# ScalarE's copies of gathered rows placed later, an expert's first two tiles transposed on TensorE, and the gate weights loaded first on their queue

## The chip, the cores and the metric

The kernel runs on one core of one Trainium2 chip. The metric is the device time of one execution in microseconds (us). Engines: TensorE (PE) multiplies and transposes, VectorE (DVE) and ScalarE (ACT) work element by element, GpSimd (POOL) pools early batches and issues gathers and scatters, SyncE (SP) issues DMAs. Each runs its own list of instructions strictly in order; they wait for each other through semaphores.

## The reference, cut to what matters

```python
k_p = k.reshape(B, H, Sp, 8, D).mean(axis=3)          # B = 8 batches, H = 8 heads, S = 576 rows, D = 64
v_p = v.reshape(B, H, Sp, 8, D).mean(axis=3)
attn = softmax(scale * q @ k_p.T);  a = attn @ v_p    # per batch and head
x = a.transpose(0, 2, 1, 3).reshape(4608, 512)
logits = x @ w_gate                                   # 8 experts
# greedy: (token, expert) pairs by falling logit; a token goes to the first expert
# with room for it, 576 tokens each
for e in range(8):
    out[mask_e] = np.maximum(x[mask_e] @ w1[e], 0.0) @ w2[e]    # w1 512 x 1024, w2 1024 x 512
```

## The kernel before, in words

**Attention.** The 4608 rows are 36 tiles of 128. For a tile, PE forms the scores (`st_s`, L229), transposes the exponentials (`st_e`, L258) and multiplies them with the values (`st_av`, L271). Keys and values of a batch are pooled beforehand: for batch 0 by PE and DVE, for the others by POOL (L174 to L178 for keys, L187 to L197 for values). Beside the pooled values stands a block of logits: `prep_v` transposes the sums of values (L210) and ACT copies them as `vT` (L212), `prep_g` multiplies `vT` with the gate weights `wblk` (L219), and DVE puts the product into `vblk` (L220). So every attention tile needs `wblk` through its batch's `prep_g`. `wblk` is 44 KB; its load is the last step of `local()` (L114, L115), on ACT's DMA queue, behind ACT's setting of constants. The rows go to `xd` in DRAM.

**Routing.** For one expert after another a search finds which tokens it takes: rounds of DVE comparing (L601), PE counting (L644), DVE diagonal and count (L648, L652), PE (L656), DVE (`g`, L663), PE (L670), DVE (`up`, L672). At the end of a search come the rows as indices (L740). The rounds are laid among the products of the expert before, at places that a planner chooses; since PE and DVE run in order, a round that is late stops what stands behind it.

**Experts.** An expert takes 576 tokens, four tiles of 128 and one of 64. Each fp32 factor is split in a high and a low part (`xh`, `xl`, `w1h`, `w1l`, `hh`, `hl`, `w2h`, `w2l`; ACT rounds the high part, DVE subtracts), and three products stand for one. Stage 1 (L1081) goes over the 8 blocks of 128 hidden columns twice: for tokens 0 to 255, then for tokens 256 to 575; a block is 12 matmuls, after which ACT takes `hh` (L1086), in the second pass `hr` too (L1088), and DVE takes `hl` (L1089). Stage 2 (L1115) has four tiles of 24 matmuls and a half tile (L1120); ACT evicts them as `yt` (L1129) and `yh` (L1133), POOL scatters them (L1095). ACT also makes `w1h` (L1033) and `w2h` (L1043) in eight pieces each, DVE `w1l` (L1037) and `w2l` (L1046).

**Gathered rows.** An expert's rows come from `xd` by POOL's indirect DMA, one per tile (`fetch`, L996), and must be transposed. For expert 0 they land in `xg` and PE transposes them, four transposes a tile (L1057), from whose PSUM tile `tp` ACT takes `xh` (L1059) and DVE `xl` (L1061). For experts 1 to 7 they land in one of three buffers `xa`; ACT copies them to `xg` with their 16-bit halves apart (`split`, L1004), SP transposes that by DMA back into `xa` (L1006), ACT puts the halves together (`join`, L1013), and then come `xh` (L1025, ACT) and `xl` (L1026, DVE).

**What sets the order.** `experts()` writes the program while it keeps an estimated clock `now`, in us. `at(after, f)` puts a step on the list `moves`, which `move(until)` empties in turn as the clock reaches each; `later` does the same for DVE. `gather` plans splits and joins at fixed distances from the moment the rows are known: splits 0 to 2 at 5.0 + 1.3t, joins 0 to 2 at 11.0 + 1.3t, the fetches of tiles 3 and 4 with joins 0 and 1, splits 3 and 4 at 13.0 + 1.3t, joins 3 and 4 at 20.0 + 1.3t. `turns` and `turn` place `xh` and `xl` of a tile from 20.0 + 1.5t on. For experts 3 to 7 the rows are known during stage 1 of the expert before; for expert 1 this is during stage 2 of expert 0.

Of the kernel before, what the change touches and what calls it, by code (L numbers as in the profile page):

```python
# [9 lines left out]
F32 = mybir.dt.float32  # L10
# [13 lines left out]
class Attention:  # L24
# [44 lines left out]
    def local(self, loc, full, consts, more, then):  # L69
        nc = self.nc  # L70

        self.kblk = [loc.tile([128, 4, 144], F32, name=f"kblk{i}") for i in range(4)]
        nc.gpsimd.memset(self.kblk[0], 0.0)

        row = loc.tile([128, 1], I32, name="row")
        nc.gpsimd.iota(row, pattern=[[0, 1]], base=0, channel_multiplier=1)
        edges = loc.tile([128, 16], F32, name="edges")
        at = []
        n = 0
        for _, heads in self.CHUNKS:  # L80
            at.append(n)
            for e in (*(h[1] for h in heads), heads[-1][2]):
                nc.gpsimd.memset(edges[:, n:n + 1], float(e))
                n += 1
        rowf = loc.tile([128, 1], F32, name="rowf")
        nc.vector.tensor_copy(rowf, row)
        nc.vector.tensor_tensor(edges, rowf.to_broadcast([128, 16]), edges, op=OP.is_ge)
        self.mask = loc.tile([128, 11], F32, name="mask")
        for c, n in enumerate(at):
            b0, b1 = self.BLOCKS[c:c + 2]  # L90
            nc.vector.tensor_tensor(self.mask[:, b0:b1], edges[:, n:n + b1 - b0], edges[:, n + 1:n + 1 + b1 - b0],
                                    op=OP.subtract)

        ones = loc.tile([128, 11], F32, name="ones8")
        nc.vector.tensor_scalar(ones, self.mask, 8.0, None, op0=OP.mult)
        small = loc.tile([128, 1], F32, name="small")
        nc.vector.tensor_scalar(small, rowf, 127.0, 8e-9, op0=OP.is_ge, op1=OP.mult)
        for b in (slice(0, 2), slice(3, 5), slice(6, 9), slice(10, 11)):
            nc.vector.tensor_scalar(ones[:, b], ones[:, b], small, None, op0=OP.add)

        self.eTs = [loc.tile([128, 5, 128], F32, name=f"eT{i}") for i in range(3)]
        for t in self.eTs:
            nc.scalar.activation(t[96:], full[96:, None, :].to_broadcast([32, 5, 128]), AF.Copy)
        self.vblk = [loc.tile([128, 11, 73], F32, name=f"vblk{i}") for i in range(4)]
        for t in self.vblk:
            nc.scalar.activation(t[:, :, 72], ones, AF.Copy)
        for t in self.kblk[1:]:
            nc.scalar.activation(t.rearrange("p j (a y) -> p (j a) y", a=2), full[:, None, :72].to_broadcast([128, 8, 72]),
                                 AF.Copy, scale=0.0)
        consts()  # L110
        then()
        more()

        self.wblk = loc.tile([128, 88], F32, name="wblk")  # L114
        nc.scalar.dma_start(self.wblk, self.wb)  # L115

    def load_k(self, b, halves=(slice(0, 4),)):
        self.rk[b] = self.raw.tile([128, 4, 8, 72], F32, name="rawk", bufs=3)
# [806 lines left out]
class Experts:  # L925
# [46 lines left out]
    def rows_of(self, t):  # L972
        return min(128, self.cap - 128 * t)

    def gather(self, rows, at=None):

        self.xg = self.buf("xg", [128, 5, 512])
        if at is None:
            for t in range(5):
                self.fetch(rows, t, self.xg[:, t])  # L980
            return
        self.xa = self.buf("xa", [128, 3, 512])
        for t in range(3):
            self.fetch(rows, t, self.xa[:, t])
            at(5.0 + 1.3 * t, lambda t=t: self.split(t))
        for t in range(2):
            at(11.0 + 1.3 * t, lambda t=t: (self.join(t), self.fetch(rows, t + 3, self.xa[:, t])))
        at(13.6, lambda: self.join(2))
        for t in range(3, 5):
            at(13.0 + 1.3 * t, lambda t=t: self.split(t))  # L990
        for t in range(3, 5):
            at(20.0 + 1.3 * t, lambda t=t: self.join(t))

    def fetch(self, rows, t, to):
        n = self.rows_of(t)
# [192 lines left out]
def experts(ctx, tc, g, R, xd, w1, w2, out, ident, cap, keep):  # L1188
# [13 lines left out]
    def later(after, t, f):  # L1202

        waiting.append((now + after, t, f))

    moves = []

    def at(after, f):
# [14 lines left out]
    def step(e):  # L1223
# [5 lines left out]
        if what == "id":  # L1229

            if p > e or p and pieces[p - 1].l < 8:
                held.append((p, crit, t, what))
                return False
            X.load_1(R.eid, 0, 4 if p else 2)
            eids[p] = R.eid
        elif what == "rows":
            if p and turned[p - 1] < 5:
                held.append((p, crit, t, what))
                return False
            X.gather(R.rows, at if p else None)  # L1240
            toks[p] = R.rows, R.halves
            turned[p] = 0
        since[p, what] = now
# [46 lines left out]
    def turn(e, t, name="tp", bufs=2):  # L1290

        nonlocal now
        if e:
            now = max(now, since[e, "rows"] + 20.0 + 1.5 * t)
            move(since[e, "rows"] + (11.0, 12.3, 13.6, 23.9, 25.2)[t])
            flush(1)
            X.xt_joined(t, later)
        else:
# [7 lines left out]
    def turns(e, upto, t0):  # L1306

        nonlocal last
        t = turned.get(e, 5)
        if t < upto and due(e, "rows", 20.0 + 1.5 * t if e else 6.5 + 1.3 * t) and now >= last + 1.4:  # L1310
            last = now
            turn(e, t)

# [158 lines left out]
```

## Time and profile before

| | |
|---|---|
| time, median of 3 runs (lowest to highest) | 625.4 us (624.82 to 625.49) |
| the profiled execution's own time | 625.91 us |
| its span, first to last instruction | 624.1 us |
| mean granted TensorE clock in it | 0.973 |
| attention | about 0 to 135 us |
| routing of expert 0, with PE mostly idle | about 139 to 163 us |
| experts | about 165 us to the end |

The profile is of one execution. A row of a timeline gives start, duration, engine, line, operation, the tiles written and read, and how many such instructions follow each other; in brackets stands how long the engine was idle before it, and what ended that. Durations of successive instructions overlap a little, so that the distance between starts is what an instruction takes of its engine. `PEld` is the loading of weights, which runs beside PE; an engine's name with a q is the part that issues DMAs and waits. A row of the windows gives, for a stretch of time, each engine's busy time and instructions, then the granted TensorE clock (1.00 is full speed), the busy share of the DMA engines and GB/s. A row of the chain gives start, duration, and what the end of the program was then waiting for. All lines are those of the kernel before.

### The profile page before, as it was taken

What the parts mean: (1) busy time and instruction counts of PE and PEld (TensorE: products, weight loads), DVE (VectorE), ACT (ScalarE), POOL (GpSimd) and SP (SyncE); (2) the same over time, 40 slices, a digit from 0 to 9 for tenths busy, and PEclk for the clock granted to TensorE, in tenths of its full rate; (3) what the DMA queues carried; (4) which work ended last, traced back from release to release, by engine and by line L of the source; (5) the groups of instructions that cost most, each with busy time, mean ns of one, the idle gap of its engine ahead of it and who ended that gap; (6) DMA issues with size and microseconds to landing.
All of it is one profiled execution on the core that took longest, in us unless ns stands there. A gap on an engine that the chain in (4) does not pass through costs nothing.

```text
span 624.1 us, 11279 instructions
## 1 busy us (share of the span) xinstructions
PE 585.8 (94%) x4155; PEld 509.4 (82%) x4155; DVE 394.1 (63%) x1149; ACT 305.0 (49%) x624; POOL 175.3 (28%) x219
## 2 busy tenths in 40 slices
PE   7899999995799989999899989998999999999994
PEld 5899999884498769878877987897789889979972
DVE  7477777888886677877674776377647616615300
ACT  7244444442353475663844294248327925925310
POOL 2999998000300420322102211111212111120021
PEclk9799999996899989999999989999999999999997
DMA  8999982121640873637611941383156228314011
GB/s 355 421 379 356 396 304 86 69 78 59 211 137 1 264 201 102 179 91 252 170 43 52 328 95 42 107 287 72 50 212 195 60 100 301 80 52 162 2 43 39
DMA packets 65986, 100.38 MB, mean 161 GB/s; under 512 B 36848, under 2 KB 36864, under 8 KB 63232
## 3 DMA queue, kind: packets, MB, share of 16 engines
q1 hardware_dynamic: 54672, 71.18, 34.6%
q0 software_dynamic: 5920, 18.89, 8.6%
q10 hardware_dynamic: 5328, 9.48, 4.1%
q8 instruction: 35, 0.57, 0.4%
q14 instruction: 31, 0.25, 0.1%
HBM read 72.40 MB, written 18.87 MB: 146 GB/s over the span
## 4 chain that ended last, share of the span: by engine, by line
PE 71%; issue 10%; DMA 7%; ACT 5%; DVE 3%; POOL 1%; POOLq 0%; another core or an unknown queue 0%; SPq 0%; DVEq 0%; ACTq 0%
PE h L1115 23%; PE h L1081 22%; PE psa L271 8%; PE pss L229 6%; DMA xa<-xd,rows 3%; PE h L1120 3%; PE pse L258 2%; ACT xg L1004 2%; PE rt L258 1%; DMA wblk<-in_moe_w_gate_dram 1%; DMA xg<-xd,rows 1%; PE rt L219 1%; PE rt L644 1%; ACT hh L1086 1%; PE rt L505 1%
## 5 line engine op out<-in xcount | busy, mean ns | idle before, releaser
L1115 PE MATMUL h<-w2l,hh 128*128 128x512 f32 x256 | 101.8, 398 | 0.0
L1115 PE MATMUL h<-w2h,hl 128*128 128x512 f32 x256 | 101.6, 397 | 0.0
L1115 PE MATMUL h<-w2h,hh 128*128 128x512 f32 x256 | 100.6, 393 | 0.3 <-PEq L1179 0.3
L1081 PE MATMUL h<-xh,w1h 128*128 128x320 f32 (+1 forms) x512 | 93.3, 302 | 2.6 <-ACT xh L1025 2.0
L1081 PE MATMUL h<-xl,w1h 128*128 128x320 f32 (+1 forms) x512 | 95.3, 303 | 0.0
L1081 PE MATMUL h<-xh,w1l 128*128 128x320 f32 (+1 forms) x512 | 91.0, 300 | 0.0
L1086 ACT ACTIVATE hh<-h 128x320 fp32r<-128x320 f32 (+1 forms) x128 | 53.0, 416 | 77.0 <-PE h L1081 68.9
L1095 POOL DMA_INDIRECT out_dram<-yt,rows x29 | 29.2, 1006 | 200.0 <-ACT yt L1129 199.6
L1089 DVE SCALAR_TENSOR_TENSOR hl<-h,hh 128x320 fp32r<-128x320 f32 (+1 forms) x128 | 57.5, 453 | 42.6 <-ACT hr L1088 23.3
L1081 PEld LDWEIGHTS h<-xh,w1h 128*128 128x128 f32 x512 | 76.4, 192 | 6.1 <-issue 3.1
L1081 PEld LDWEIGHTS h<-xl,w1h 128*128 128x128 f32 x512 | 77.8, 192 | 2.3 <-issue 2.3
L1081 PEld LDWEIGHTS h<-xh,w1l 128*128 128x128 f32 x512 | 76.6, 192 | 0.1
L996 POOL DMA_INDIRECT xa<-xd,rows x35 | 35.1, 1002 | 135.0 <-ACT xg L1013 64.4
L1129 ACT ACTIVATE yt<-h 128x512 f32<-128x512 f32 x32 | 19.2, 599 | 96.9 <-PE h L1115 62.5
L271 PE MATMUL psa<-vblk,eT 128*128 128x146 f32 (+3 forms) x400 | 63.0, 305 | 0.0
L1026 DVE TENSOR_TENSOR xl<-xg,xh 128x512 fp32r<-128x512 f32 (+1 forms) x35 | 22.0, 630 | 54.1 <-ACT xh L1025 54.1
L1115 PEld LDWEIGHTS h<-w2h,hh 128*128 128x128 f32 x256 | 48.2, 188 | 9.6 <-issue 0.7
L1115 PEld LDWEIGHTS h<-w2h,hl 128*128 128x128 f32 x256 | 48.2, 188 | 9.0
L1115 PEld LDWEIGHTS h<-w2l,hh 128*128 128x128 f32 x256 | 48.4, 189 | 8.6
L271 PEld LDWEIGHTS psa<-vblk,eT 128*128 128x128 f32 (+1 forms) x400 | 53.1, 182 | 1.8 <-issue 0.3
L1046 DVE TENSOR_TENSOR w2l<-raw,w2h 128x512 fp32r<-128x512 f32 x64 | 43.2, 682 | 5.8 <-ACT w2h L1043 5.8
L1004 ACT ACTIVATE xg<-xa 128x1024 uint16<-128x1024 uint16 (+1 forms) x35 | 36.8, 1064 | 19.7 <-DMA xa<-xd,rows 18.6
(215 smaller groups left out, 957.3 us busy)
## 6 DMA issues: line engine op xcount, KB each, us to landing
raw<-in_moe_w_dram SPq DMA_DIRECT2D x64, 512.0 KB
xd<-xt ACTq DMA_DIRECT2D x36, 256.0 KB
rawv<-in_v_dram SPq DMA_DIRECT2D x7, 1280.0 KB
rawk<-in_k_dram SPq DMA_DIRECT2D x7, 1152.0 KB
rawq<-in_q_dram SPq DMA_DIRECT2D x7, 1152.0 KB
rawk<-in_k_dram SPq DMA_DIRECT2D x2, 576.0 KB
rawv<-in_v_dram SPq DMA_DIRECT2D x1, 768.0 KB
rawq<-in_q_dram SPq DMA_DIRECT2D x1, 640.0 KB
```

What stands on the lines that cost most here:

```text
L229: nc.tensor.matmul(ps[cols, j // 2, 144 * (j % 2):144 * (j % 2) + 144], self.q_of(b, j, n, cols.stop - cols.start), self.kblk[b % 4][:, j] ...
L271: self.nc.tensor.matmul(o[h], self.eT[i][:, c, h], self.vblk[b % 4][:, self.BLOCKS[c]:self.BLOCKS[c + 1]], start=(c == cs[0]), stop=(c == ...
L996: self.nc.gpsimd.indirect_dma_start(out=to[:n], out_offset=None, in_=self.xd, in_offset=bass.IndirectOffsetOnAxis(ap=rows[:n, t:t + 1], ax ...
L1004: nc.scalar.activation(xs.rearrange("p (s d) -> p s d", s=2), self.xa[:n, t % 3].bitcast(U16).rearrange("p (d s) -> p s d", s=2), AF.Copy)
L1026: later(0.9, 0.7, lambda: self.nc.vector.tensor_tensor(xl, x, xh.bitcast(F32), op=OP.subtract))
L1046: self.nc.vector.tensor_tensor(self.w2l[:, i], self.raw2[e][:, i], self.w2h[:, i].bitcast(F32), op=OP.subtract)
L1081: nc.tensor.matmul(ps[:, :m], a[:, j, fs], b[:, j, o], start=(n == 0), stop=(n == 11))
L1086: nc.scalar.activation(hh[:, f, o], ps[:, :m], AF.Relu)
L1089: later(0.65, 0.4, lambda f=f, o=o, m=m, ps=ps: nc.vector.scalar_tensor_tensor(hl[:, f, o], ps[:, :m], 0.0, hh[:, f, o].bitcast(F32), op0= ...
L1095: st = nc.gpsimd.indirect_dma_start(out=rows, out_offset=bass.IndirectOffsetOnAxis(ap=idx, axis=0), in_=y, in_offset=None)
L1115: nc.tensor.matmul(ps, a[:, f, o], b[:, f], start=(f == 0 and k == 0), stop=(f == 7 and k == 2))
L1129: self.nc.scalar.activation(y, ps, AF.Copy)
```

## The change

Three parts.

1. The tile `wblk` and its load move from the end of `local()` to its beginning.
2. `gather` is given the tiles that go `direct`: all five for expert 0, tiles 0 and 1 for expert 1, none for the others. Direct tiles are fetched into `xg` and transposed on PE. So expert 1 has eight more transposes on PE, and two splits, two DMA transposes and two joins fewer; its tiles 2 to 4 take the three buffers `xa`, and its five fetches are issued one behind the other.
3. For experts 2 to 7 splits 0 to 2 are planned at 10.0 + 1.4n, splits 3 and 4 at 25.0 and 26.5, and every join 6.5 behind its split. `joined` gives the time from which `xh` and `xl` of a tile may follow, and `turn` empties the list of planned steps up to that time. For expert 1 the three splits stand at 12.0 + 1.4n.

```diff
     def local(self, loc, full, consts, more, then):
         nc = self.nc
+
+        self.wblk = loc.tile([128, 88], F32, name="wblk")
+        nc.scalar.dma_start(self.wblk, self.wb)
...
         more()
 
-        self.wblk = loc.tile([128, 88], F32, name="wblk")
-        nc.scalar.dma_start(self.wblk, self.wb)
...
-    def gather(self, rows, at=None):
+    def gather(self, rows, direct=range(5), at=None):
 
         self.xg = self.buf("xg", [128, 5, 512])
-        if at is None:
-            for t in range(5):
-                self.fetch(rows, t, self.xg[:, t])
-            return
-        self.xa = self.buf("xa", [128, 3, 512])
-        for t in range(3):
-            self.fetch(rows, t, self.xa[:, t])
-            at(5.0 + 1.3 * t, lambda t=t: self.split(t))
-        for t in range(2):
-            at(11.0 + 1.3 * t, lambda t=t: (self.join(t), self.fetch(rows, t + 3, self.xa[:, t])))
-        at(13.6, lambda: self.join(2))
-        for t in range(3, 5):
-            at(13.0 + 1.3 * t, lambda t=t: self.split(t))
-        for t in range(3, 5):
-            at(20.0 + 1.3 * t, lambda t=t: self.join(t))
+        for t in direct:
+            self.fetch(rows, t, self.xg[:, t])
+        rest = [t for t in range(5) if t not in direct]
+        if rest:
+            self.xa = self.buf("xa", [128, 3, 512])
+        for t in rest[:3]:
+            self.fetch(rows, t, self.xa[:, t % 3])
+        plan = []
+        for n, t in enumerate(rest):
+            first = n < 3
+            begin = (10.0 if len(rest) > 3 else 12.0) + 1.4 * n if first else 25.0 + 1.5 * (n - 3)
+            plan.append((begin, lambda t=t: self.split(t)))
+            plan.append((begin + 6.5, lambda t=t: self.join(t)))
+            if first and n + 3 < len(rest):
+                plan.append((begin + 6.5, lambda t=rest[n + 3]: self.fetch(rows, t, self.xa[:, t % 3])))
+        for after, f in sorted(plan, key=lambda x: x[0]):
+            at(after, f)
+
+    @staticmethod
+    def joined(e, t):
+
+        return (26.0 - 1.5 * 3 + 1.5 * t if t > 2 else 10.0 + 1.4 * t) + 7.5 if e > 1 else 12.0 + 1.4 * (t - 2) + 7.5
...
+    def direct(e):
+        return range(5) if e == 0 else range(2) if e == 1 else range(0)
...
-            X.gather(R.rows, at if p else None)
+            X.gather(R.rows, direct(p), at)
...
-        if e:
-            now = max(now, since[e, "rows"] + 20.0 + 1.5 * t)
-            move(since[e, "rows"] + (11.0, 12.3, 13.6, 23.9, 25.2)[t])
+        if t not in direct(e):
+            now = max(now, since[e, "rows"] + X.joined(e, t))
+            move(now)
             flush(1)
...
-        if t < upto and due(e, "rows", 20.0 + 1.5 * t if e else 6.5 + 1.3 * t) and now >= last + 1.4:
+        if t < upto and due(e, "rows", 6.5 + 1.3 * t if t in direct(e) else X.joined(e, t)) and now >= last + 1.4:
```

How this moves instructions is shown at three places, all on ACT, whose rows PE and DVE wait for. Line numbers are each kernel's own: in the changed kernel the same statement stands 1 to 11 lines later (split L1012, join L1021, `xh` L1033 or from PSUM L1067, `w1h` L1041, `hh` L1094, `hr` L1096, `w2h` L1051, `yt` L1137, `yh` L1141). A number behind a tile's name is its buffer.

The first place is the start of the program on ACT, whose first rows set constants (`eT`, `vblk`, `kblk`). Before, the load of `wblk` stands behind all of them:

```order
L108 ACTIVATE kblk_131<-ones 128x576
L447 ACTIVATE j_190<-i_186 128x1152
L151 ACTIVATE kblk_128<-psa 64x72 x2
L483 ACTIVATE blk<-i_186 128x648
L484 ACTIVATE blk<-i_186 128x72
L115 DMA wblk<-in_moe_w_gate_dram 128x88
L241 ACTIVATE e<-e 128x576
```

In the changed kernel it is the first instruction behind the program's opening branch, ahead of the loading of ACT's table:

```order
L1479 UNCONDITIONAL_BRANCH
L73 DMA wblk<-in_moe_w_gate_dram 128x88
L106 ACT_TABLE_LOAD
L106 ACTIVATE eT_171<-ones 32x640
L106 ACTIVATE eT_172<-ones 32x640
```

Nothing else moves there, on ACT or on the other engines.

The second place is stage 2 of expert 0 on ACT, where expert 1's rows arrive. Before, behind two evictions `yt`:

```order
L1129 ACTIVATE yt<-h 128x512 x2
L1004 ACTIVATE xg<-xa 128x1024 x3
L1129 ACTIVATE yt<-h 128x512
L1033 ACTIVATE w1h<-raw_2602 128x512 x2
L1013 ACTIVATE xg<-xa 128x2x512
L1033 ACTIVATE w1h<-raw_2602 128x512
L1013 ACTIVATE xg<-xa 128x2x512 x2
L1129 ACTIVATE yt<-h 128x512
L1033 ACTIVATE w1h<-raw_2602 128x512
L1004 ACTIVATE xg<-xa 128x1024
L1004 ACTIVATE xg<-xa 64x1024
L1133 ACTIVATE yh<-h 128x256
```

In the changed kernel, from the same evictions on:

```order
L1137 ACTIVATE yt<-h 128x512 x2
L1067 ACTIVATE xh<-tp 128x4x128 x2
L1137 ACTIVATE yt<-h 128x512
L1041 ACTIVATE w1h<-raw_2602 128x512 x2
L1012 ACTIVATE xg<-xa 128x1024
L1041 ACTIVATE w1h<-raw_2602 128x512
L1012 ACTIVATE xg<-xa 128x1024
L1012 ACTIVATE xg<-xa 64x1024
L1137 ACTIVATE yt<-h 128x512
L1041 ACTIVATE w1h<-raw_2602 128x512
L1021 ACTIVATE xg<-xa 128x2x512
L1033 ACTIVATE xh<-xg 128x4x128
```

Two `xh` from PE's transposes stand where three splits stood; the splits of tiles 2 to 4 come between the pieces of `w1h`. Behind these rows follow `yh`, the join of tile 3, two `w1h`, the join of tile 4, `xh`, `hh`, `w1h`, `xh`, `w1h`. On PE the first four transposes stand behind the 15th L1115 that follows L755 of expert 0's stage 2, the next four five L1115 later.

The third place is stage 1 of expert 2 on ACT, at its change from the first pass (`hh` of 256 columns) to the second (320), where expert 3's rows arrive; the same holds one and two experts later. Before:

```order
L1043 ACTIVATE w2h<-raw_3695 128x512 x2
L1004 ACTIVATE xg<-xa 128x1024
L1086 ACTIVATE hh<-h 128x256
L1043 ACTIVATE w2h<-raw_3695 128x512
L1004 ACTIVATE xg<-xa 128x1024
L1086 ACTIVATE hh<-h 128x320
L1088 ACTIVATE hr<-h 128x64
L1004 ACTIVATE xg<-xa 128x1024
L1043 ACTIVATE w2h<-raw_3695 128x512
L1086 ACTIVATE hh<-h 128x320
```

In the changed kernel:

```order
L1051 ACTIVATE w2h<-raw_3699 128x512 x2
L1094 ACTIVATE hh<-h 128x256
L1051 ACTIVATE w2h<-raw_3699 128x512
L1094 ACTIVATE hh<-h 128x320
L1096 ACTIVATE hr<-h 128x64
L1051 ACTIVATE w2h<-raw_3699 128x512
L1094 ACTIVATE hh<-h 128x320
L1096 ACTIVATE hr<-h 128x64
L1012 ACTIVATE xg<-xa 128x1024
L1051 ACTIVATE w2h<-raw_3699 128x512
L1094 ACTIVATE hh<-h 128x320
L1096 ACTIVATE hr<-h 128x64
```

The first split moves behind three more `hh` and two more `w2h`; joins 0 to 2 follow between the last four `hh`, and splits 3 and 4 move behind the last of them, into stage 2. The orders of PE, DVE and SP are the same there as before; POOL's fetches of tiles 3 and 4 move with the joins.

## The prediction

> **What bounds the kernel now.** I read the page first: one engine is busy nearly all the time.
>
> ```profile
> span 624.1 us, 11279 instructions
> ...
> PE 585.8 (94%) x4155; PEld 509.4 (82%) x4155; DVE 394.1 (63%) x1149; ACT 305.0 (49%) x624; POOL 175.3 (28%) x219
> ```
>
> TensorE (PE) does the same products before and after, so a change can shorten the run only where PE idles or runs at half clock. PE's timeline lists its instructions, with the idle time ahead of each in brackets. These gaps lie where the change acts:
>
> ```profile
> 17.32 1.43 PE L219 MATMUL psa<-wblk,vT 128*128 128x40 f32 x6 [3.22 <-DMA wblk<-in_moe_w_gate_dram]
> 217.47 0.18 PE L656 MATMUL rt<-cnt,fold 128*128 128x8 f16 x1 [0.81 <-DVE cnt L652]
> 227.62 0.38 PE L1081 MATMUL h<-xh,w1h 128*128 128x256 f32 x1 [2.04 <-ACT xh L1025]
> 306.12 0.39 PE L644 MATMUL rt<-oh,cmp 128*128 128x32 bf16 x9 [1.49 <-DVE cmp L601]
> 312.80 0.17 PE L670 MATMUL rt<-g,ones 128*128 128x8 bf16 x1 [1.09 <-DVE g L663]
> 364.32 0.39 PE L644 MATMUL rt<-oh,cmp 128*128 128x32 bf16 x9 [1.99 <-DVE cmp L601]
> 421.86 0.39 PE L644 MATMUL rt<-oh,cmp 128*128 128x32 bf16 x9 [1.38 <-DVE cmp L601]
> 428.55 0.17 PE L670 MATMUL rt<-g,ones 128*128 128x8 bf16 x1 [1.09 <-DVE g L663]
> ```
>
> Together they are 13.1 us of PE's some 38 us of idle time. Then I read the busy times by window, for the third column from the end, PEclk, the clock granted to PE (behind it the DMA engines' busy share and GB/s):
>
> ```profile
> 10.00:20.00 10.00, 6.70 (x44) 6.21 (x44) 4.97 (x8) 4.01 (x12) 5.74 (x6) 0.83 1.02 424
> 20.00:30.00 10.00, 10.00 (x72) 9.60 (x72) 5.60 (x10) 3.51 (x8) 9.63 (x9) 0.83 1.01 419
> 220.00:230.00 10.00, 7.96 (x67) 5.18 (x67) 6.98 (x22) 7.40 (x12) 3.57 (x5) 0.91 0.58 138
> 230.00:240.00 10.00, 10.00 (x85) 9.91 (x84) 7.44 (x19) 6.01 (x12) 0.00 (x0) 0.92 0.54 193
> 360.00:370.00 10.00, 8.01 (x52) 7.65 (x52) 7.92 (x19) 10.00 (x20) 2.12 (x3) 0.83 0.55 119
> 420.00:430.00 10.00, 7.52 (x59) 6.99 (x58) 7.42 (x19) 10.00 (x21) 2.10 (x3) 1.00 0.42 93
> ```
>
> At half clock for t us, a 10 us window shows 1 - 0.05t. So 0.83 is 3.4 us: two such windows at 10 to 30 (6.8 us), 1.8 + 1.6 = 3.4 us at 220 to 240, 3.4 us at 360 to 370. Each lies behind a gap of 3.22, 2.04 or 1.99 us; behind 1.38 us the window at 420 stays at 1.00. While PE is busy, 3.4 us at half clock costs half of it, 1.7 us.
>
> Here a rule of the Trainium skill differs (TensorE: Matmul & The Clock Gate, Part 1): the clock falls back to half only after an idle window of about 3.4 us. By it the gaps of 2.04 and 1.99 us would leave the clock alone, and the sum below would be 2 x 1.7 us smaller. The rows show half clock behind both, so I go by the rows.
>
> **Part A, the gate weights.** Read: ScalarE's (ACT's) and GpSimd's (POOL's) timelines, and the chain of waits.
>
> ```profile
> 8.97 0.22 ACT L151 ACTIVATE kblk<-psa 64x72 f32<-64x72 f32 x1 [1.61 <-PE psa L148]
> 9.08 0.38 ACTq L115 DMA_DIRECT2D wblk<-in_moe_w_gate_dram  x1
> 14.13 0.49 ACT L212 ACTIVATE vT<-psa 128x384 f32<-128x384 f32 x1
> ```
>
> ```profile
> 9.08 8.11 DMA wblk<-in_moe_w_gate_dram
> 18.75 2.11 PE pss L229 x8
> 24.12 0.98 PE pss L229 x8
> 27.03 1.13 PE pss L229 x16
> 35.15 0.58 PE rt L219 x6
> ```
>
> ```profile
> 19.50 1.63 POOL L178 TENSOR_TENSOR kblk<-tk 64x288 f32<-64x288 f32 x2
> ```
>
> Moved to the head of ACT's queue, the load is issued about 8.3 us earlier. Even with the same 8.11 us it lands near 9, before vT, the other operand of L219, at 14.62. So L219 can start near 14.67, 2.65 us earlier. The half clock that follows goes too: from 17.32 to 27.03 (tile 4's scores) PE takes 9.71 us; at full clock these are L219's 0.58 and two tiles of 27.03 - 24.12 = 2.91, so 6.4, which saves 3.3. (The same eight L229 took 2.11 at half clock and 0.98 at full.) Sum 5.95, which puts tile 4 at 21.1. It needs the keys of batch 1, and POOL finishes these at 19.50 + 1.63 = 21.13: a cap near 5.85. Its queries come over DMA engines that the windows show full (1.02, 1.01); no row gives their landing. I take **5.3**, between 2.65 (the clock stays half) and 5.85, near the top because both terms have rows. The cost: ACT's issue, 0.38 us, now precedes its first copies; the 1.61 us idle ahead of 8.97 hides it, else it is 0.38. SP's loads keep their order.
>
> **Part B, expert 1's first two tiles.**
>
> ```profile
> 167.60 0.60 PE L1057 MATMUL tp<-ident,xg 128*128 128x128 f32 x4
> 167.95 0.36 PE L1081 MATMUL h<-xh,w1h 128*128 128x256 f32 x1
> ```
>
> ```profile
> 206.31 2.14 PE h L1115 x9
> 208.45 0.05 PE rt L755
> 236.43 3.68 PE h L1081 x30
> ```
>
> ```profile
> 212.41 2.95 ACT L1004 ACTIVATE xg<-xa 128x1024 uint16<-128x1024 uint16 x3 [3.33 <-DMA xa<-xd,rows]
> 231.17 0.63 ACT L1033 ACTIVATE w1h<-raw 128x512 fp32r<-128x512 f32 x1
> 231.69 1.38 ACT L1013 ACTIVATE xg<-xa 128x1024 uint16<-128x1024 uint16 x1
> 233.10 0.63 ACT L1025 ACTIVATE xh<-xg 128x512 fp32r<-128x512 f32 x1
> 233.64 0.61 ACT L1033 ACTIVATE w1h<-raw 128x512 fp32r<-128x512 f32 x1
> ```
>
> Removed: ACT's split of three tiles stands ahead of its w1h copies, so DVE was late for L656 (0.81), and stage 1 waited 2.04 for tile 1's xh, with 1.7 of half clock behind it. Two splits, two joins and two queued transposes go; the gaps' causes go with them: **+4.55**.
>
> Added on PE: two groups of four transposes; 167.60 to 167.95 is 0.35 a group, **-0.7**. The first group stands 15 products behind L755, at 208.5 + 15 x 0.238 (2.14 / 9) = 212.0; ACT's row shows the first gathered tile there at 212.4: a wait of 0.4 to **0.5** (0 if an undivided queue is quicker, 1.5 if the second tile is late too). The third to fifth gathers now go ahead of one scatter on POOL; nobody waits for that scatter.
>
> Added on ACT: L1120 ends at 227.62 - 2.04 = 225.6, now about 226.0 (+0.7 +0.5 -0.8). Then ACT does yh, join 3, two w1h, join 4, xh, hh, w1h, xh, w1h. Start to start in the rows, w1h is 0.52, a join 1.41 (half-size about 0.8), xh 0.54; so 226.0 + 0.3 + 1.41 + 1.04 + 0.8 + 0.54 + 0.3 + 0.52 + 0.3 + 0.52 = 231.7 for the last w1h. DVE has a comparison and two w1l to do behind that (about 0.75 each, an estimate from the 0.75 of L601 below): near 234.0. PE takes 3.68 / 30 = 0.123 a product, so column block 4 begins at 226.0 + 48 x 0.123 + 0.25 of L644 = 232.2 and wants the last w1l near 233. I take a new wait of **1.1** (0 to 2). Sum of B: 4.55 - 0.7 - 0.5 - 1.1 = **2.25** (0.5 to 3.8).
>
> **Part C, experts 3 to 5.** Read: ACT's and DVE's (VectorE's) timelines, and the chain.
>
> ```profile
> 293.58 6.85 DMA xa<-xd,rows
> ```
>
> ```profile
> 300.51 1.06 ACT L1004 ACTIVATE xg<-xa 128x1024 uint16<-128x1024 uint16 x1 [3.04 <-DMA xa<-xd,rows]
> ```
>
> ```profile
> 301.87 0.43 DVE L1089 SCALAR_TENSOR_TENSOR hl<-h,hh 128x256 fp32r<-128x256 f32 x1 [2.43 <-ACT hh L1086]
> 305.31 0.75 DVE L601 TENSOR_TENSOR cmp<-q16a,j 128x1152 bf16<-128x1152 f16 x1
> 312.20 0.49 DVE L1089 SCALAR_TENSOR_TENSOR hl<-h,hh 128x320 fp32r<-128x320 f32 x1 [1.08 <-ACT hr L1088]
> ```
>
> The gather takes 6.85 us, ACT asks for it 3.04 us early and stands; hh behind it is late, DVE waits 2.43 for hh, its comparison ends at 306.06, PE waits 1.49. Later ACT is still full, DVE waits 1.08 for hr, and g is 1.09 late. Now the first split stands three hh and two w2h later, near 302, behind the landing at 300.43: ACT does not stand. Splits 3 and 4, 1.06 each, leave this stretch for stage 2. Of ACT's 17 us from 298 to 315 the 3.04 and two of 1.06 go, some 5, while PE's own work there is 17 - 1.49 - 1.09 = 14.4 us; so hh keeps up, with 1.5 to 2 us in hand at cmp and g. PE's and DVE's orders stay. All five gaps go, 1.49 + 1.09 + 1.99 + 1.38 + 1.09 = 7.04, and the half clock at 364 with them, 1.7: **8.75**. Bounds: 3.5 (half of each gap comes back, and one half clock) and 8.75. Late next are tiles 3 and 4, joined some 33 us behind the rows of 293, near 326; the next expert's second column half wants them, and that begins some 7 us ahead of the gap at 364 (as 298 does ahead of 306): covered by 30 us.
>
> **Sum.** 5.3 + 2.25 + 8.75 = 16.3. The profiled execution took 625.9 us (span 624.1 and 1.8 around it), 0.5 above the median of the runs, 625.4: 625.9 - 16.3 = **609.6 us**.
>
> **The rivals.**
> 1. *Part A is capped by supply.* Tile 4 waits for batch 1's queries, and PE's gain ends there: 2.65 instead of 5.3, 612.3 us. For it: DMA at 1.02, POOL at 9.63 of 10. Against: before, the chain passes 27.03 without a wait, which shows only that they were not late then. Chance 0.12.
> 2. *ACT stays full in part C.* Joins, each 1.41, now stand between hh of late blocks; g comes late again and half the gain goes: C 4.4, 614.0 us. For it: ACT 10.00 of 10 at 360. Against: 5 us less to do. Chance 0.13.
> 3. *The clock gates again at expert 1.* If wait and transposes reach some 2 us of missing products, 3.4 us at half clock: B 0.55, 611.3 us. The skill bears on it (same page, Part 4): transposes do not count as PE-busy for the gate. Then 0.5 + 0.7 = 1.2 us counts as idle, under the 1.38 that left the clock up, so it decides only from a gather 0.8 us later. Chance 0.08.
> 4. *The half clock is not the gaps' doing.* By the skill's Part 1 it would not follow gaps of 2 us; if something else sets it there, 2 x 1.7 stay: 613.0 us. Against: both stretches begin with the gap. Chance 0.04.
> 5. *Slower.* In each of the six expert changes from 1 to 7, a join reached before its transpose stops ACT with hh behind it; once hh is 3.5 us late (its 1.5 in hand and 2.0 of gap), PE loses 2.0 and 1.7 of half clock, 3.7 x 6 = 22 us: 609.6 + 22 = 631.8. For it: in ACT's order three joins of each expert now stand between hh of its late blocks. Against: by plan a join comes 6.5 us after its split, where it came 6.0 after before. Chance 0.03.
>
> The forecast has the remaining 0.60, with its own range 606.5 to 612. **Range** 605.5 to 617: below, A and B at their best, 5.85 + 3.8 + 8.75 = 18.4, give 607.5, and 2 us are left for short waits not counted; above, rivals 1 and 2 together give 616.6. A measurement of this kernel tells about 0.2%, 1.25 us, from no change; only rival 5 lies there or beyond, and half of two parts failing at once: faster 0.95, same 0.02, slower 0.03.
>
> **What would show it.** In the profile after: L219 starting near 14.7 with clock 1.00 from 10 to 30; no wait of ACT for gathered rows from 290 on; no gap above 0.4 us at L644 and L670 in experts 2 to 4 and clock 1.00 there; L1081 of expert 1 starting without its 2.04 us; a wait near 1 us for w1l five blocks on. It is wrong if any of those gaps returns at its place, if tile 4's scores wait 2 us or more for queries or keys, or if ACT waits at L1013.

## The result, and the profile after

The changed kernel takes 609.63 us (median of 4 runs, 609.18 to 610.18), the kernel before beside it 625.11 us (4 runs, 624.09 to 625.49): a ratio of 0.9755, 95% interval 0.9738 to 0.9772. The forecast was 609.6. The profiled execution took 610.03 us, its own 0.4 above the forecast. The sum was right; its terms were less so, as the stages show. Two executions among the experiments, at 657.96 us (a variant of the changed kernel) and 3219.41 us (the kernel before), were far slower than all others and are left out of the medians.

The page of the changed kernel, its span and its busy times:

```profile
span 608.2 us, 11281 instructions
...
PE 582.0 (96%) x4163; PEld 504.7 (83%) x4163; DVE 393.8 (65%) x1149; ACT 302.3 (50%) x620; POOL 175.3 (29%) x219
```

PE's timeline of the changed kernel, where the eight gaps stood (L220 was L219, L1065 was L1057, L1089 was L1081, L645 was L644):

```profile
15.40 0.84 PE L220 MATMUL psa<-wblk,vT 128*128 128x40 f32 x6 [0.58 <-ACT vT L213]
208.38 0.66 PE L1065 MATMUL tp<-ident,xg 128*128 128x128 f32 x4 [0.55 <-DMA xg<-xd,rows]
208.79 0.48 PE L1123 MATMUL h<-w2h,hh 128*128 128x512 f32 x1
230.85 0.38 PE L1089 MATMUL h<-xh,w1l 128*128 128x256 f32 x1 [0.88 <-DVE w1l L1045]
306.60 0.39 PE L645 MATMUL rt<-oh,cmp 128*128 128x32 bf16 x9
```

L220 now waits 0.58 us, and for `vT` instead of the gate weights. The two new waits that the forecast put at 0.5 and 1.1 us are there, 0.55 for the gather and 0.88 for `w1l`. At L645 and L671 no gap is left in experts 2 to 4. One of the signs that the prediction named for being wrong did appear, and cost PE nothing: ACT waited at a join, for expert 7's rows, in stage 2 of expert 6, where PE has no gap.

```profile
534.46 1.99 ACT L1021 ACTIVATE xg<-xa 128x1024 uint16<-128x1024 uint16 x2 [1.31 <-DMA xa<-xg]
```

The windows of the same trace, with PEclk third from the end:

```profile
10.00:20.00 10.00, 9.34 (x74) 8.78 (x74) 6.49 (x10) 6.16 (x16) 5.61 (x6) 1.00 1.02 426
220.00:230.00 10.00, 9.97 (x95) 8.41 (x91) 7.90 (x22) 7.37 (x15) 1.60 (x3) 1.00 0.72 247
300.00:310.00 10.00, 10.00 (x69) 8.92 (x69) 8.37 (x24) 10.00 (x21) 2.11 (x3) 1.00 0.55 93
360.00:370.00 10.00, 10.00 (x64) 7.49 (x62) 6.92 (x23) 7.82 (x13) 2.25 (x4) 1.00 0.33 81
```

And, for comparison, one of these windows in the kernel before:

```profile
300.00:310.00 10.00, 8.51 (x66) 8.15 (x65) 6.83 (x17) 9.49 (x19) 1.58 (x2) 1.00 0.49 99
```

The clock is full in all four windows of the changed kernel. From 300 to 310 both PE and ACT (fourth of the busy times) are at 10.00, where ACT had 9.49 before: ACT has no less to do there, and PE no longer waits. So it was not ACT's load that held PE.

Where the time went is read from PE's starts in the two profiled executions, stage by stage:

| PE starts | before | after | shift | this stage | forecast |
|---|---|---|---|---|---|
| first scores (L229) | 8.70 | 9.42 | +0.72 | +0.72 | 0 |
| stage 1 of expert 0 | 165.71 | 160.76 | -4.95 | -5.67 | -5.3 (A) |
| stage 2 of expert 0 | 195.91 | 191.74 | -4.17 | +0.78 | 0 |
| stage 1 of expert 2 | 284.79 | 279.22 | -5.57 | -1.40 | -2.25 (B) |
| stage 1 of expert 6 | 510.75 | 494.88 | -15.87 | -10.30 | -8.75 (C) |

From expert 6 on nothing changes. Part C gave 1.55 us more than forecast, A 0.4 more; B gave 0.85 less, and two stages in which PE's instructions are the same before and after took 1.5 back.

### The profile page after: what moved, and what is told of

Read it like the earlier page. It is cut to its first block, busy times and chain, and to the rows that moved or that the text cites. A ratio compares the mean times of both kernels' runs of the same rounds, so it can differ in the third digit from the quotient of the medians.

```text
span 608.2 us, 11281 instructions
## 1 busy us (share of the span) xinstructions
PE 582.0 (96%) x4163; PEld 504.7 (83%) x4163; DVE 393.8 (65%) x1149; ACT 302.3 (50%) x620; POOL 175.3 (29%) x219
## 4 chain that ended last, share of the span: by engine, by line
PE 81%; issue 7%; DVE 4%; DMA 3%; ACT 1%; POOL 1%; POOLq 0%; another core or an unknown queue 0%; SPq 0%; DVEq 0%
PE h L1089 30%; PE h L1123 25%; PE psa L272 8%; PE pss L230 6%; PE h L1128 4%; DMA xg<-xd,rows 2%; PE pse L259 2%; PE rt L259 1%; PE rt L506 1%; PE rt L220 1%; PE rt L645 1%; PE rt L607 1%; DMA out_dram<-yt,rows 1%; DMA raw<-in_moe_w_dram 1%; PE rt L211 1%
## 5 line engine op out<-in xcount | busy, mean ns | idle before, releaser
L1094 ACT ACTIVATE hh<-h 128x320 fp32r<-128x320 f32 (+1 forms) x128 | 52.9, 414 | 85.7 <-PE h L1089 85.3
L1089 PE MATMUL h<-xl,w1h 128*128 128x320 f32 (+1 forms) x512 | 93.8, 300 | 0.0
L1089 PE MATMUL h<-xh,w1l 128*128 128x320 f32 (+1 forms) x512 | 90.9, 298 | 0.9 <-DVE w1l L1045 0.9
L1089 PE MATMUL h<-xh,w1h 128*128 128x320 f32 (+1 forms) x512 | 91.4, 298 | 0.3 <-ACT xh L1067 0.3
L1089 PEld LDWEIGHTS h<-xh,w1h 128*128 128x128 f32 x512 | 75.2, 189 | 3.5 <-issue 2.7
L1089 PEld LDWEIGHTS h<-xl,w1h 128*128 128x128 f32 x512 | 76.8, 190 | 0.0
L1089 PEld LDWEIGHTS h<-xh,w1l 128*128 128x128 f32 x512 | 75.8, 190 | 1.1 <-DVE w1l L1045 1.1
L1004 POOL DMA_INDIRECT xa<-xd,rows x33 | 32.6, 989 | 129.7 <-ACT xg L1021 64.4
L1137 ACT ACTIVATE yt<-h 128x512 f32<-128x512 f32 x32 | 19.2, 601 | 93.9 <-PE h L1123 57.0
L1034 DVE TENSOR_TENSOR xl<-xg,xh 128x512 fp32r<-128x512 f32 (+1 forms) x33 | 20.7, 628 | 57.6 <-ACT xh L1033 57.6
L1045 DVE TENSOR_TENSOR w1l<-raw,w1h 128x512 fp32r<-128x512 f32 x64 | 41.4, 687 | 10.5 <-ACT w1h L1041 10.3
```

Source lines behind the costliest of these rows:

```text
L1004: self.nc.gpsimd.indirect_dma_start(out=to[:n], out_offset=None, in_=self.xd, in_offset=bass.IndirectOffsetOnAxis(ap=rows[:n, t:t + 1], ax ...
L1034: later(0.9, 0.7, lambda: self.nc.vector.tensor_tensor(xl, x, xh.bitcast(F32), op=OP.subtract))
L1045: self.nc.vector.tensor_tensor(l, raw, h.bitcast(F32), op=OP.subtract)
L1089: nc.tensor.matmul(ps[:, :m], a[:, j, fs], b[:, j, o], start=(n == 0), stop=(n == 11))
L1094: nc.scalar.activation(hh[:, f, o], ps[:, :m], AF.Relu)
```

## The experiments

The theory is the prediction's: each part takes away waits of PE in a stage of its own. The rivals are that the parts act on each other, that ACT's load and not its standing was the cause in part C, and that the half clock has another cause than the gaps. Each kernel is told with the median of its runs; the kernel before took 625.3 to 625.6 us beside them.

**Part A alone.** The kernel before with the load of `wblk` first:

```diff
+        self.wblk = loc.tile([128, 88], F32, name="wblk")
+        nc.scalar.dma_start(self.wblk, self.wb)
...
-        self.wblk = loc.tile([128, 88], F32, name="wblk")
-        nc.scalar.dma_start(self.wblk, self.wb)
```

> Part A alone on the kernel before. Theory (the parts act in separate stages; the stage starts of the two traces give each its share): the attention ends some 5 us earlier, expert 0 may give 0.8 of it back, all later gaps stay as before: 620.0 to 621.0 us against 625.1. The row of L219 starts near 15 us and the clock stays at 1.00 from 10 to 30 us. Rival (the load's early issue also delays the start: the first scores came 0.72 us later after the change because ACT's issue and the shared DMA engines hold back the first keys): the same, but the first scores start at 9.4 us again. Second rival (the 0.72 is the phase in which the clock comes up): the first scores start anywhere from 8.7 to 9.4 us, by how long the 13 warming matmuls took.

Measured: 621.18 us against 625.29, ratio 0.9939 (0.9915 to 0.9962); first scores at 9.10. Part A is worth some 4 us (2.4 to 5.3 by the interval), less than the 5.67 of its stage; the reason is told under part A below. The first scores lie between the two values, which speaks for the phase of the clock; the next runs settle that.

**Part B undone**, with the old distances for expert 1 and no direct tiles:

```diff
-        return range(5) if e == 0 else range(2) if e == 1 else range(0)
+        return range(5) if e == 0 else range(0)
...
+        if old:
+            for t in range(3):
+                at(5.0 + 1.3 * t, lambda t=t: self.split(t))
...
-            X.gather(R.rows, direct(p), at)
+            X.gather(R.rows, direct(p), at, p in (1,))
```

> The changed kernel with part B undone: expert 1's five tiles go through the buffers again, at the old distances. Theory by the stage starts of the two traces: part B is worth 1.4 us, so 611.0 us against 609.6. By the prediction's own ledger 2.25 us: 611.9. Rival (the eight transposes, the wait for the gather and the new wait for w1l eat the gain): 609.6 or less. In the trace the waits of 0.8 us at the count and 2.0 us at the start of stage 1 of expert 1 are back, with the half clock behind.

Measured: 610.86 us, so part B is worth 1.2 us, near the stage's 1.40 and well under the ledger's 2.25. The gap at the start of expert 1's stage 1 is back at its old size, but in this execution no half clock lies behind it. PE's timeline and the window, in the kernel without part B:

```profile
222.99 0.38 PE L1100 MATMUL h<-xh,w1h 128*128 128x256 f32 x1 [2.04 <-ACT xh L1044]
```

```profile
220.00:230.00 10.00, 7.80 (x72) 6.99 (x69) 8.72 (x23) 8.01 (x15) 1.08 (x1) 1.00 0.81 248
```

The same two rows in the kernel with part A alone show the same gap with 3.4 us of half clock behind it:

```profile
223.81 0.39 PE L1082 MATMUL h<-xh,w1h 128*128 128x256 f32 x1 [2.04 <-ACT xh L1026]
```

```profile
220.00:230.00 10.00, 7.80 (x57) 6.64 (x56) 7.40 (x20) 7.33 (x14) 1.11 (x2) 0.83 0.78 231
```

So one and the same gap of 2.04 us brings the clock down in one execution and not in another: of the five traces that have it, three show half clock behind it.

**Part C alone**: the kernel before with the new distances for experts 2 to 7. **Part C undone**: the changed kernel with the old distances for these (the edit as above, with other experts named).

> Part C alone on the kernel before. Theory: 10.3 us by the stage starts (2.9 + 0.2, 3.7, 2.8 + 0.2, 0.5 in the changes from expert 2 to 6): 614.8 us. By the prediction's ledger 8.75: 616.4. Rival (the gain hangs on the parts before it, which shift these stages against the DMA traffic): under 8 us, over 617.

> The changed kernel with part C undone: parts A and B alone. Theory: 609.6 + 10.3 = 619.9 us, and the waits at L644 and L670 of experts 2 to 4 are back at 1.0 to 2.0 us each, ACT standing some 3 us for gathered rows. Rival (part C is not what took them away, but the shift by the other parts): 612 or less.

Measured: part C alone 614.45 us, part C undone 619.64 us. So C is worth 10.8 us on the kernel before and 10.0 us on the changed one; A (4.1), B (1.2) and C (about 10.4) make 15.7 of the 15.5 measured for all three. The parts add up within the 1 to 2 us that such medians leave open, and nothing here speaks for the rival that they act on each other. With C undone PE waits 1.23, 1.62 and 1.92 us at L645 for the three experts, and 1.09 at L671 for the first two: close to before, with the longest wait at another expert.

**What in part C does it?** Two kernels change one thing each in the changed kernel. The first plans splits 0 to 2 early again and leaves splits 3 and 4 late:

```diff
-            begin = (10.0 if len(rest) > 3 else 12.0) + 1.4 * n if first else 25.0 + 1.5 * (n - 3)
+            begin = (5.0 if len(rest) > 3 else 12.0) + 1.4 * n if first else 25.0 + 1.5 * (n - 3)
```

> The changed kernel, but for experts 2 to 7 splits 0 to 2 are planned at 5.0 + 1.4n again (joins 6.5 behind them); splits 3 and 4 stay late, at 25.0 and 26.5. Theory (what cost time was ACT standing for the gathered rows, with hh behind it): ACT waits about 3 us at the first split of experts 3 to 5, the waits of PE at L645 return at about 1.5, 2.0 and 1.4 us, some 5 us in all: 614.5 to 615.5 us, and up to 1.7 more for each gap after which the clock falls. Rival (what cost time was the sum of ACT's work in this stretch; the two splits moved out of it have cured that): ACT may stand, but PE waits under 0.5 us each time: under 611.5 us.

Measured: 619.44 us. All of part C is gone: more than the theory's 614.5 to 615.5, and more than the 617.2 that it allows with the one fall of the clock in this trace. ACT's first row and PE's next waits in this kernel:

```profile
295.40 1.06 ACT L1012 ACTIVATE xg<-xa 128x1024 uint16<-128x1024 uint16 x1 [3.07 <-DMA xa<-xd,rows]
```

```profile
301.01 0.39 PE L645 MATMUL rt<-oh,cmp 128*128 128x32 bf16 x9 [1.52 <-DVE cmp L602]
307.70 0.17 PE L671 MATMUL rt<-g,ones 128*128 128x8 bf16 x1 [1.09 <-DVE g L664]
```

ACT stands 3.07 us, and both waits return at the size of before, that of `g` too, although splits 3 and 4 are out of the stretch. The prediction had credited their going with part of the cure. The second kernel tests that from the other side, with 20.0 in place of 25.0 for splits 3 and 4:

> The changed kernel, but for experts 2 to 7 splits 3 and 4 are planned at 20.0 and 21.5 instead of 25.0 and 26.5. Their rows are fetched with joins 0 and 1, at 16.5 and 17.9, and a gather took 6.9 us from issue to landing, so ACT reaches split 3 some 3 us too early. Theory (ACT standing costs what stands behind it): ACT waits 2 to 4 us there, the last hh and hr of stage 1 are late, and PE waits 0.5 to 2 us at L645, L671 or the start of stage 2 of experts 2 to 4: 612 to 615 us. Rival (late blocks have the five banks of PSUM as slack): ACT stands, PE does not: 609 to 610.5 us.

Measured: 610.34 us, and no gap of PE at L645 or L671. ACT waited only 0.6 us in all for gathered rows, not 2 to 4: my estimate of when it reaches the split was wrong, so this kernel hardly tests standing there. It shows that when splits 3 and 4 are copied is worth under 1 us.

**How much room there is.** Splits 0 to 2 half way, at 7.5 in place of 10.0:

> The changed kernel, but for experts 2 to 7 splits 0 to 2 are planned at 7.5 + 1.4n, half way between 5.0 and 10.0 (joins 6.5 behind them). In the changed kernel the first split is reached about 1 us after the rows have landed. Theory (it counts by how much ACT stands beyond its slack): ACT stands some 1.5 us at each first split of experts 3 to 5; hh has 1.5 to 2 us in hand, so PE waits at most 0.5 us each: 609.5 to 611 us. Rival (any wait of ACT there passes on in full): 1.5 us each at L645 and more at L671, 614 us or more.

Measured: 612.84 us, between the theory and the rival, and neither had the mechanism. ACT stands 0.72 us instead of 1.5, and the wait comes later, at the next round:

```profile
302.02 0.64 ACT L1051 ACTIVATE w2h<-raw 128x512 fp32r<-128x512 f32 x1
302.53 0.46 ACT L1094 ACTIVATE hh<-h 128x320 fp32r<-128x320 f32 x1
302.85 0.26 ACT L1096 ACTIVATE hr<-h 128x64 f32<-128x64 f32 x1
302.95 2.63 ACT L1021 ACTIVATE xg<-xa 128x1024 uint16<-128x1024 uint16 x2
305.38 0.47 ACT L1094 ACTIVATE hh<-h 128x320 fp32r<-128x320 f32 x1
```

```profile
306.00 0.49 DVE L1097 SCALAR_TENSOR_TENSOR hl<-h,hh 128x320 fp32r<-128x320 f32 x1 [1.71 <-ACT hr L1096]
```

```profile
307.69 0.39 PE L645 MATMUL rt<-oh,cmp 128*128 128x32 bf16 x9 [0.77 <-DVE cmp L602]
```

Two joins now stand next to each other (2.63 us) ahead of one `hh`; DVE waits 1.71 us for the `hr` behind it, its comparison is late, PE waits 0.77. In the changed kernel each join has an `hh` on either side. That is rival 2 of the prediction, joins among `hh`, and it is real: it decides when two of them meet.

**Is the half clock the gap's doing?** The kernel before, with the gap ahead of the first L219 filled by idle matmuls; the load stays late:

```diff
             if n == 2:
+                warm(12)
                 self.prep_g(0)
```

> The kernel before, with 12 idle matmuls of ones put on PE ahead of the first L219, into the 3.2 us that PE waits for the gate weights; they compute nothing that is used. The load is as late as before. Theory (the clock falls when PE idles for about half of a window of 3.4 us): with the gap filled the clock stays at 1.00 from 10 to 30 us, tile 4's scores come 6.4 us after L219 starts instead of 9.7, and the time is 622.0 us against 625.3. Rival (the half clock there has another cause, or an idle window of all 3.4 us is needed): the clock shows 0.83 as before and the time is within 1 us of the kernel before.

Measured: 622.65 us (10 runs, 620.56 to 626.11) against 625.47, ratio 0.9959 (0.9936 to 0.9982), a gain of 1.1 to 4.0 us. The chain in this kernel from L219 to tile 4's scores, and the window:

```profile
17.43 0.81 PE psa L219 x6
24.20 1.19 PE pss L229 x16
```

```profile
10.00:20.00 10.00, 9.63 (x67) 7.54 (x67) 5.61 (x9) 4.56 (x13) 5.57 (x6) 1.00 1.03 427
```

L219 starts no earlier than before (17.32), yet tile 4 follows after 6.77 us instead of 9.71, at full clock: filling the gap with nothing saved 2.9 us there. The profiled execution lost them again, and took 625.0 us, because PE then stood for expert 0's gathered rows:

```profile
162.03 1.12 PE L1058 MATMUL tp<-ident,xg 128*128 128x128 f32 x4 [3.52 <-DMA xg<-xd,rows]
```

The half clock behind L219 was the gap's doing, and the rival falls. One trace alone could not show that, since a gap does not bring the clock down every time; the ten runs and the windows of the last section say the same.

**A version that beats both.** The changed kernel's two new waits are attacked: expert 1's joins of tiles 3 and 4 go behind the last `w1h`, its transposes a little later on PE.

```diff
-            plan.append((begin + 6.5, lambda t=t: self.join(t)))
+            meet = begin + 6.5 if len(rest) > 3 or n == 0 else 24.5 + 1.5 * n
+            plan.append((meet, lambda t=t: self.join(t)))
...
-            now = max(now, since[e, "rows"] + 6.0 + 1.3 * t) + 0.45
+            now = max(now, since[e, "rows"] + (6.8 if e else 6.0) + 1.3 * t) + 0.45
```

> The changed kernel with its two new waits attacked: expert 1's joins of tiles 3 and 4 come at 26.0 and 27.5 instead of 19.9 and 21.3, behind the last w1h; its first transposes on PE come 0.8 us of planned time later. Theory: the wait of 0.88 us for w1l and of 0.55 for the gather go, with the 0.15 each that the pipeline takes to fill again: 608.0 us against 609.6. Rival (the next wait is right behind, in the routing round that DVE does there): 609.0 to 609.6. In the trace no gap over 0.3 us from 200 to 250 us.

Measured: 608.20 us (608.10 to 608.63, 5 runs), ratio to the kernel before 0.9729 (0.9707 to 0.9751). Its two windows from 220 to 240 us:

```profile
220.00:230.00 10.00, 10.00 (x98) 8.99 (x94) 8.52 (x25) 6.86 (x15) 1.21 (x1) 1.00 0.69 249
230.00:240.00 10.00, 10.00 (x84) 9.71 (x83) 8.60 (x29) 5.56 (x15) 0.00 (x0) 1.00 0.36 117
```

PE has no gap there. The changed kernel, run again unaltered, gave the value to set it against:

> The changed kernel once more, unaltered, beside the two that follow on the same chip. Theory (few of its gaps reach half of a clock window, so its time hardly depends on the phase in which the windows fall): 609.2 to 610.2 us again, a spread of 1 us against the 4 us of the kernel before; PE's row of the 13 warming matmuls and the first scores shift by up to 1.3 us from run to run, with the moment at which the clock comes up. Rival (the spread of before has another source, which the changed kernel shares): 3 us or more between its runs.

Measured: 609.60 us (609.17 to 609.95, 5 runs), beside 623.82 to 627.39 for 9 runs of the kernel before. So the better version gains 1.4 us more. The changed kernel spreads over 0.8 us where the kernel before spreads over 3.6, which fits the theory that the spread came with the long gaps. Not all of it need have: the kernel with 20.0, which has no long gap either, ranged from 609.74 to 611.91.

**A miss.** Idle matmuls in the routing of expert 0, on top of the better version:

```diff
             if not early:
                 ps = self.psum()
+                if not spare and shadow is not None:
+                    self.warm(3, ps)
```

> The kernel of e7_best, with three idle matmuls of ones ahead of the counts of rounds 2 to 4 of expert 0's search, into the 0.9 us that PE waits for each comparison; they compute nothing that is used. Theory (small matmuls and waits together leave the clock at half there, and the counts take 1.36 us at half clock): the clock stays higher from 139 to 150 us, each count ends some 0.3 to 0.5 us earlier, expert 0 starts about 1 us earlier: 607.2 us against 608.2. Rival (the comparisons set the pace, or the idle matmuls themselves are late at half clock): 608.0 to 609.5.

Measured: 610.00 us, 1.8 slower than without (the runs of both stand beside different runs of the kernel before, with medians of 625.6 and 625.5). PE's rows say why, first one from the better version, then two from this kernel:

```profile
145.58 1.36 PE L607 MATMUL rt<-oh,cmp 128*32 128x8 bf16 x36 [0.86 <-DVE cmp L602]
```

```profile
142.51 1.44 PE L506 MATMUL rt<-ones 128*128 128x512 bf16 x3 [0.27 <-DVE up L675]
143.87 1.36 PE L607 MATMUL rt<-oh,cmp 128*32 128x8 bf16 x36
```

The clock was already at half, so three idle matmuls took 1.44 us in a gap of 0.9 and pushed the counts, which still took 1.36. A filling must fit its gap at half clock, or come before the clock falls.

## Why the prediction was right, and where its terms were not

**The mechanisms held.** Seven of the eight gaps went and the first shrank from 3.22 to 0.58 us, for the reasons given: the early load, the transposes on PE, ACT asking for gathered rows once they are there. The rivals that would have ended slower, or kept half of part C, did not come true.

**What was counted as certain and is chance: the half clock.** Of the 16.3 us, about 3 in part A, 1.7 in part B and 1.7 in part C are half clock behind a gap. The one trace before showed it all three times; other executions, with the same code at these places, do not always.

**Part A, 5.3 forecast, 5.67 in its stage.** L220 started 0.73 us later than the forecast's 14.67, because PE's first scores were late by 0.72. Counted from these, tile 4's scores came 5.56 us earlier than before ((27.03 - 8.70) - (22.19 - 9.42), with 22.19 from the chain after), between the 5.3 that I took and the cap of 5.85.

```profile
22.19 1.13 PE pss L230 x16
```

But the kernel with part C alone, whose load is as late as before, waits 2.28 us, and the clock stays full:

```profile
16.18 0.81 PE L221 MATMUL psa<-wblk,vT 128*128 128x40 f32 x6 [2.28 <-DMA wblk<-in_moe_w_gate_dram]
```

```profile
22.95 1.13 PE pss L231 x16
```

```profile
10.00:20.00 10.00, 7.39 (x58) 6.86 (x57) 6.32 (x10) 4.63 (x13) 5.77 (x6) 1.00 1.02 425
```

From its first scores (8.21) tile 4's scores come after 14.74 us, against 18.33 before and 12.77 after. In such an execution part A is worth 2.0 us, in the other kind 5.6; the 4.1 of the medians lie between. The six runs of part C alone spread accordingly, from 610.93 to 615.84 us.

The cap of rival 1 is real, but it comes from the queries and lies later than the 21.13 that the prediction took from the keys. PE met it where its first scores were early: with part C undone for 0.19 us, and in the second run of the changed kernel for 0.51. The rows of these two:

```profile
21.87 1.17 PE L230 MATMUL pss<-kblk,rawq 128*64 128x144 f32 x14 [0.19 <-DMA rawq<-in_q_dram]
```

```profile
21.99 1.17 PE L230 MATMUL pss<-kblk,rawq 128*64 128x144 f32 x14 [0.51 <-DMA rawq<-in_q_dram]
```

**The start, 0 forecast, +0.72.** The forecast hid ACT's issue under 1.61 us of idle time, and this was right; what moved is the 13 warming matmuls ahead of the first scores. They are the same in all kernels. The row in part C alone, in the kernel with splits 3 and 4 at 20.0, and in the second run of the changed kernel:

```profile
1.98 4.43 PE L507 MATMUL rt<-ones 128*128 128x512 bf16 x13 [1.98 <-DVE ones L433]
```

```profile
1.97 5.73 PE L506 MATMUL rt<-ones 128*128 128x512 bf16 x13 [1.97 <-DVE ones L432]
```

```profile
1.98 4.37 PE L506 MATMUL rt<-ones 128*128 128x512 bf16 x13 [1.98 <-DVE ones L432]
```

They took 5.15 us in the trace before, 5.73 in the first of the changed kernel and 4.37 in its second: the same program, 1.36 us apart. The first scores follow them (9.42 and 8.04 us). So this term is chance, not a cost of the change.

**Expert 0, 0 forecast, +0.78.** The change leaves these orders alone. PE waited for expert 0's own gathered rows in every trace, for other tiles and times in each; the two traces of the changed kernel differ there as well. From stage 1 to stage 2 of expert 0 the thirteen traces take 29.97 to 31.72 us (30.20 before, 30.98 after). That it varies is shown, what sets it is open.

**Part B, 2.25 forecast, 1.40 in its stage, 1.2 by the medians.** The added terms were right: 0.41 us for a group of transposes (208.38 to 208.79, forecast 0.35), waits of 0.55 and 0.88 (forecast 0.5 and 1.1). The step that failed is the 1.7 us of half clock "behind the gap" in the 4.55: the kernel without part B has the gap and no half clock, so it is lost in some executions only. From stage 2 of expert 0 to stage 1 of expert 2, PE took 88.88 us before (284.79 - 195.91) and 87.48 after; without part B and without half clock 87.77 (278.96 - 191.19). In such an execution part B is worth 0.3 us, in the other kind 1.4. And where the half clock does come, it costs less than 1.7: with it the stretch takes 88.88 us before, 89.26 with part A alone and 89.18 with the filled gap at L219; without it 87.77, and 87.72 with part C alone. That is 1.1 to 1.5 us. In the pair of traces this explains some 0.6 of the missing 0.85; the rest was not followed up.

**Part C, 8.75 forecast, 10.30 in its stages.** The cause was right, its list of costs too short. A gap costs more than its bracket, as PE's rows before show:

```profile
303.74 0.75 PE L1081 MATMUL h<-xl,w1h 128*128 128x320 f32 x4
304.32 0.31 PE L1081 MATMUL h<-xh,w1h 128*128 128x320 f32 x1
```

Four matmuls start 0.58 us from the next, 0.145 each, so without a gap the next would have started at 304.47. It started at 306.12: 1.65 us lost, where the bracket, which counts from the modelled end at 304.63, says 1.49. If each of the five gaps costs 0.16 more, that is 0.8 in all; and in expert 5, whose gap of 0.29 us I had left out, PE gained 0.54. With these 8.75 becomes 10.1. The 1.7 of half clock in the 8.75 is chance here too, but the sum hardly hangs on it: with part A alone the gap at that place is 1.62 us, the clock stays up, and a wait of 1.09 at L671 stands where the trace before has none. From expert 2 to expert 6 that kernel takes 225.63 us, the kernel before 225.96, the changed one 215.66. One reason in the working was wrong without harm: that splits 3 and 4 leave the stretch. In the kernel with 5.0 they have left it, and with the early splits, and ACT standing at them, all five gaps return.

The errors, +0.72, +0.78, -0.37, +0.85 and -1.55, nearly cancel, to 0.43 in the profiled execution. That the median hit the forecast is luck; each term was good to some 0.4 to 1.6 us.

## What to carry to other kernels

An engine that runs in order must not reach an instruction before its data: look where it stands, count what is queued behind, and move the request to where the data have landed, not the work to another engine. Price a gap of TensorE start to start, and add half a clock window only as a chance if it exceeds some 1.7 us. After moving copies, look whether two long ones now stand side by side ahead of something that a third engine waits for.

## What the runs showed of the hardware

In the experts' stages the granted clock falls for 3.4 us at a time. It fell behind gaps of PE of 2.04, 1.99, 1.92 (part C undone, third expert) and also 1.71 us (the kernel with 5.0, second expert), and, with the 3.22 at L219, for 6.8 us. It stayed up behind every gap of 1.62 us or less and, in other executions, behind 2.04 and, at the place of L219, behind 2.28. The routing of expert 0, where PE has little to do, and its first stage are left out. The row and the windows around the 1.71:

```profile
358.82 0.39 PE L645 MATMUL rt<-oh,cmp 128*128 128x32 bf16 x9 [1.71 <-DVE cmp L602]
```

```profile
350.00:360.00 10.00, 8.29 (x63) 8.04 (x62) 7.17 (x19) 6.79 (x14) 0.00 (x0) 0.99 0.68 181
360.00:370.00 10.00, 10.00 (x63) 9.32 (x63) 7.49 (x23) 8.35 (x19) 1.93 (x3) 0.84 0.15 41
```

Why the same gap counts in one execution and not in another can be read from the traces. Within each trace the moments at which the clock changes lie whole multiples of 3.413 us apart, so the grid of windows can be carried on from any of them. With part A alone the clock is low from 225.67 to 229.08; its gap of 2.04 us lies mostly in the window just before:

```profile
222.25:225.66 3.41, 1.70 (x19) 1.53 (x20) 2.30 (x6) 2.55 (x5) 1.08 (x1) 1.00 0.55 117
225.67:229.08 3.41, 3.41 (x17) 3.32 (x18) 2.65 (x6) 2.36 (x4) 0.00 (x0) 0.50 0.96 330
```

In the kernel without part B the clock comes up at 157.01, so windows begin 18 and 19 times 3.413 us later, at 218.45 and 221.87, and the second of these moments cuts the same gap in two:

```profile
218.45:221.86 3.41, 2.51 (x23) 1.22 (x19) 2.21 (x7) 2.98 (x6) 1.29 (x3) 1.00 0.56 139
221.87:225.28 3.41, 2.12 (x22) 1.96 (x23) 2.30 (x8) 2.12 (x5) 0.87 (x1) 1.00 0.53 111
225.28:228.69 3.41, 3.41 (x31) 3.37 (x30) 3.34 (x9) 3.17 (x5) 0.00 (x0) 1.00 0.91 338
```

PE (first of the busy times) is busy for 1.70 of 3.41 us where the clock falls, and for 2.51 and 2.12 where it stays. Between the first attention tiles and PE's last matmul, the routing and start of expert 0 left out, the thirteen traces have seven windows in which PE is idle for 1.71 us or more, and the clock falls behind all seven; the most that it bore is 1.62 (part A alone, from 358.78). So here a window of which half is idle sufficed. The limit is not sharp: in the first stage of expert 0 one window with 1.74 us idle, in two gaps, left the clock up (part A alone, from 164.23).

The Trainium skill (TensorE: Matmul & The Clock Gate, Part 1) says that the window runs freely and that the warm-up varies with its phase; the 4.37 to 5.73 us of the same 13 matmuls agree. It also says that an idle window of about 3.4 us is needed for the fall; here 1.71 us sufficed.
